# Softmax per head in whole-head instructions, its mask added by TensorE in the first two batches, a weight's sign by a 16-bit VectorE operation, and two PSUM banks for group 0

## The chip, the core and the metric

One core of one Trainium2 chip runs the whole program. The metric is the device time of one execution in microseconds (us). The engines are named as in the profile: PE (TensorE matmuls), PEld (its weight loads), DVE (VectorE), ACT (ScalarE), POOL (GpSimd) and SP (SyncE, which here issues every DMA).

## What is computed

Windowed attention over 8 batches, 8 heads, 576 positions and 64 values per head, then a gated MLP on all 4608 tokens. Half of the heads see the last 32 positions, the others every fourth of the last 128.

```python
scores = scale * np.matmul(q, k.transpose(0, 1, 3, 2))
rel = pos[:, None] - pos[None, :]
mask_plain = (rel >= 0) & (rel < window)
mask_dil = (rel >= 0) & (rel < window * dilation) & (rel % dilation == 0)
scores = np.where(masks[None, :, :, :], scores, -1000000000.0)
scores = scores - np.max(scores, axis=-1, keepdims=True)
attn = np.exp(scores)
attn = attn / (np.sum(attn, axis=-1, keepdims=True) + 1e-09)
x = np.matmul(attn, v)                      # then tokens x 512
h = x @ w_in                                # 512 -> 2048
g = h * (1.0 / (1.0 + np.exp(-1.702 * h)))
out = g @ w_out                             # 2048 -> 512
```

## The kernel before

The MLP runs over nine groups of 512 tokens: one for each batch (`main[0]` to `main[7]`) and one for the tails of all batches (`rest`). In each group, `up(f)` for f = 0 to 15 makes 128 of the 2048 hidden values (12 matmuls of 128x512, line 437), `tanh` on ACT (L445), `gate` on DVE (L448), `hi_g` and `lo_g` split the result into two parts, and `down(f)` adds it into four accumulators (12 matmuls, lines 473, 474 and 477). Every product is made from three: high times high, low times high, high times low. `up` writes a PSUM bank `hp`; only the first two steps of group 0 use `sp0` and `sp1` instead (L431). So `up(f+1)` has to wait until `gate` of f has read the bank.

The weights come as 64-bit floats. `decode` (L210) turns one block of them into a high and a low fp32 part: a DMA into one of five cells, three ACT instructions (`value` L235, `low` L236, `sign` L237), a shift (L239) and an add (L241) on DVE, then the high part (a copy, ACT or DVE) and the low part (a subtraction, DVE or POOL). There are 32 blocks, two for each f, and all are decoded while group 0 runs.

`attention(b, c)` handles two heads (a = 0, 1) of one batch, c = 0 to 3. `scores` (L278) makes 20 windows of 32 queries by 64 keys into a PSUM tile of 128 partitions by 5 by 64 for each head. `exponents` (L295) then runs five times for each head, on 128x64 elements: a DVE instruction that scales, adds the mask and takes the maximum (L298, with a second instruction that reads the maximum out), and an ACT Exp that also sums (L301, with a second one that reads the sum out). `weights` divides by the sum (`pr` times `sm`, DVE or POOL) and transposes on DVE; `spread` copies the result into `bt` (copies, or DMAs for batch 1 and for half of batch 0); `product` (L353) multiplies with v on PE; `drain_x` writes the tokens' vectors. Batch 0 is handled before group 0 starts, batch b + 1 beside group b.

The order is made in advance. Every piece of work is added to a `Plan` with its cost on the engines that could do it, its urgency and what it reads and writes; `ordered` (L63) then replays time with these costs and takes, at each moment, the most urgent piece that could start, on the cheapest engine that could start it. Each engine runs its part in just that order: an instruction that waits holds all that stand behind it. In the first 30 us of the plan, `warm` matmuls of zeros (L546) fill PE's planned idle time. Pools, DVE and SP follow the same list.

Of the kernel before, what the change touches and what calls it, by code (L numbers as in the profile page):

```python
# [115 lines left out]
def tile_windowed_attention_then_gated_mlp(  # L116
# [61 lines left out]
    V.memset(mask[0:32, 0, 0:32], NEG)  # L178

# [30 lines left out]
    def decode(n, urgency):  # L210
# [17 lines left out]
        freed = () if f < NF - 4 or n % 2 == 0 else ("bt1",)  # L228
        low, top = (raw.bitcast(U32).rearrange("p (n t) -> p n t", t=2)[:, :, j] for j in range(2))
        sign = raw.bitcast(F16).rearrange("p (n t) -> p n t", t=4)[:, :, 1]  # L230
# [4 lines left out]
        add({ACT: 0.56}, urgency, lambda e: A.activation(value, f32(top), AF.Copy, scale=2.0 ** -112), (R,), (E,))  # L235
        add({ACT: 0.56}, urgency, lambda e: A.activation(low, low, AF.Copy, scale=2.0 ** -29), (R,), (R + "l",))  # L236
        add({ACT: 0.56}, urgency, lambda e: A.activation(sign, f32(top), AF.Copy, scale=2.0 ** -112),  # L237
            (R,), (R + "l",))
        add({DVE: -0.335}, urgency, lambda e: V.tensor_scalar(  # L239
            out=word, in0=word, scalar1=3, scalar2=None, op0=ALU.logical_shift_left), (), (E,))  # L240
        add({DVE: -0.61}, urgency, lambda e: V.tensor_tensor(out=word, in0=word, in1=low, op=ALU.add),  # L241
            (R + "l",), (E, *freed))
        add({ACT: 0.56, DVE: -0.34}, urgency, lambda e: copy(e, hi, value), (E,), (key,))
        add({DVE: -0.61, POOL: 1.35}, urgency, lambda e: pair(e, lo, value, f32(hi), ALU.subtract), (E,), (key,))
# [4 lines left out]
    def attention(b, c, urgency):  # L249
# [4 lines left out]
        y = (i + 1) % 2 if b == 0 else 0  # L254
# [20 lines left out]
        places = [f"acc{(2 * i + a) % 4}" if b == 0 else f"sp{a}" for a in range(2)]  # L275
        chained = b >= FIRST

        def scores(e, heads):  # L278
            for a in heads:
                u["sp", a] = bank([P, QT, W], places[a], f"sp_{i}_{a}")  # L280
            for t in range(QT):
                for a, j in [(a, j) for a in heads for j in range(min(4, S // 32 - 4 * t))]:
                    g, rows = 4 * t + j, slice(D * a, D * a + D)
                    dst, keys = u["sp", a][32 * j:32 * j + 32, t], u["qk"][rows, 1]
                    for w in (0, 32) if g == 0 else (0,):
                        n = 32 if g == 0 else W
                        at = max(32 * g - 32, 0)
                        T.matmul(dst[:, w:w + n], u["qk"][rows, 0, 32 * g:32 * g + 32], keys[:, at:at + n],  # L288
                                 start=True, stop=True, tile_position=(D * a, 32 * j))

        for heads in ((0,), (1,)) if b < FIRST else ((0, 1),):
            add({PE: 0.5 * len(heads)}, urgency - 1.0e5, lambda e, heads=heads: scores(e, heads),
                (f"qk{z}", "product") if chained else (f"qk{z}",), [places[a] for a in heads], 1.0 if b else 0.0)

        def exponents(a, t):  # L295
            n = min(P, S - P * t)
            box, key = pr[0:n, a, t], f"{i % 2}{a}.{t}"
            add({DVE: 0.15}, urgency, lambda e: V.tensor_tensor_reduce(  # L298
                out=box, in0=u["sp", a][0:n, t], in1=mask[0:n, t if dil or t == 0 else QT - 1], scale=-0.125, scalar=-NEG,
                op0=ALU.add, op1=ALU.min, accum_out=mx[0:n, a, t:t + 1]), (places[a],), (f"pr{key}", f"mx{key}"))  # L300
            add({ACT: 0.33}, urgency, lambda e: A.activation(  # L301
                box, box, AF.Exp, bias=mx[0:n, a, t:t + 1], scale=-1.0, accum_out=sm[0:n, a, t:t + 1]),
                (f"mx{key}",), (f"pr{key}", f"sm{key}"))

        def weights(hs):

            n, heads = hs.stop - hs.start, range(hs.start, hs.stop)
            boxes = [f"{i % 2}{a}.{t}" for a in heads for t in range(QT)]
            sums, probs = [f"sm{k}" for k in boxes], [f"pr{k}" for k in boxes]
            for a in heads:  # L310
                for t in range(QT):
                    exponents(a, t)
# [3 lines left out]
            for a in heads:  # L316
                add({POOL: 0.69, DVE: -0.41}, urgency, lambda e, a=a: pair(
                    e, pr[:, a], pr[:, a], sm[:, a, :, None].broadcast_to([P, QT, W]), ALU.mult),
                    sums, [f"pr{i % 2}{a}.{t}" for t in range(QT)])
# [5 lines left out]
        def spread():  # L325

            for m in (4, 5, 6, 7, 0, 1, 2, 3):
# [15 lines left out]
                if b == 1 or y:  # L343
                    costs = {DMA: 82}
                else:
                    costs = {ACT: 0.49, DVE: -0.33}
                add(costs, urgency, work, [f"ct{i % 2}{prev}{a}" for a in (0, 1)], (f"bt{y}{m}", f"spread{i}.{m}"))

        for hs in (slice(0, 1), slice(1, 2)) if b < FIRST else (slice(0, 2),):
            weights(hs)  # L350
# [21 lines left out]
        def drain_x(hf):  # L372
# [35 lines left out]
    class Group:  # L408
# [20 lines left out]
        def up(self, f):  # L429
            hps = self.hps  # L430
            place = ("sp0", "sp1")[f] if self is main[0] and f < 2 else "hp"  # L431
# [31 lines left out]
            if self is main[0]:  # L463
                lows[POOL] = 1.23
# [122 lines left out]
```

## Time and profile before

| | |
|---|---|
| median of 3 runs | 927.82 us (927.69 to 929.02) |
| the profiled execution | 927.5 us |
| its span, first to last instruction | 925.6 us |
| PE busy | 901.4 us, 97% |
| DVE busy | 476.4 us, 51% |
| ACT busy | 402.0 us, 43% |
| POOL busy | 45.2 us, 5% |
| mean granted TensorE clock | 0.994 |

Shares over the whole span mix two very different parts. Up to about 161 us the weights are decoded, batch 0 and 1 are attended and group 0 runs; from there on, PE works without a gap. So the page's table by slices, and tables by stretch, are read before the shares. A busy PE is not PE at its peak: matmuls overlap, so the distance from start to start tells what one costs.

### The profile page before, as it was taken

The page shows a single profiled execution, that of the slowest core. Times are in us where ns is not written, and L with a number is a line of the kernel's source. Part 1 is how long each engine was busy: PE and PEld are TensorE (multiplying, and loading weights), DVE is VectorE, ACT ScalarE, POOL GpSimd, SP SyncE. Part 2 cuts the span into 40 slices and gives each one's busy share as a digit, 9 for nine tenths or more (in the row PEclk, how much of TensorE's full clock was granted, in tenths as well). Part 3 has the DMA queues.
Part 4 walks back from the last instruction along what each step waited for, and adds up shares of the span by engine and source line. Part 5 has one row for each costly group of instructions (what it writes and reads, how often), then busy time and mean ns, then how long its engine had stood idle before and what let it go on. Part 6 is the DMA issues. An engine that isn't in the chain of part 4 may idle for free.

```text
span 925.6 us, 17159 instructions
## 1 busy us (share of the span) xinstructions
PE 901.4 (97%) x6721; PEld 726.0 (78%) x6726; DVE 476.4 (51%) x1529; ACT 402.0 (43%) x1187; POOL 45.2 (5%) x41
## 2 busy tenths in 40 slices
PE   8798889999999999999999999999999999999997
PEld 4476676888888888888888888888888888888886
DVE  7786785656365436653656346544653333333332
ACT  6999995545255215541545144522551121122111
POOL 1023120000000000000000000000000000000000
PEclk9989999999999999999999999999999999999999
DMA  7566543121031102210221002200200010001002
GB/s 261 177 218 201 156 139 134 41 81 41 16 112 40 56 1 86 67 52 4 72 58 64 15 26 86 82 15 0 86 2 1 1 45 1 1 1 46 0 1 46
DMA packets 25185, 58.60 MB, mean 63 GB/s; under 512 B 6992, under 2 KB 8720, under 8 KB 25104
## 3 DMA queue, kind: packets, MB, share of 16 engines
q1 hardware_dynamic: 25104, 57.50, 19.2%
q8 instruction: 53, 0.87, 0.4%
q14 instruction: 28, 0.23, 0.1%
HBM read 46.14 MB, written 9.44 MB: 60 GB/s over the span
## 4 chain that ended last, share of the span: by engine, by line
PE 88%; ACT 8%; DVE 2%; POOL 1%; issue 0%; DMA 0%; DVEq 0%; ACTq 0%
PE hp_m L437 35%; PE acc_m L473 12%; PE acc_m L477 12%; PE acc_m L474 12%; PE hp_r L437 5%; PE av L361 4%; PE sp L288 3%; ACT cell L237 2%; PE acc_r L477 2%; PE acc_r L474 2%; PE acc_r L473 2%; ACT words L235 1%; ACT second L237 1%; ACT cell L236 1%; ACT pr L301 1%; ACT g_m L445 1%
## 5 line engine op out<-in xcount | busy, mean ns | idle before, releaser
L437 PE MATMUL hp_m<-xh,wih 128*128 128x512 f32 x512 | 204.8, 400 | 10.2 <-DVE g_m L448 9.5
L448 DVE SCALAR_TENSOR_TENSOR g_m<-g_m,hp_m 128x512 f32<-128x512 f32 x128 | 87.9, 687 | 240.7 <-ACT g_m L445 239.7
L473 PE MATMUL acc_m<-gh,woh 128*128 128x512 f32 x512 | 202.5, 395 | 2.9 <-DVE gh L196 2.9
L437 PE MATMUL hp_m<-xh,wil 128*128 128x512 f32 x512 | 200.3, 391 | 0.3 <-DVE wil L201 0.3
L474 PE MATMUL acc_m<-gh,wol 128*128 128x512 f32 x512 | 200.3, 391 | 0.0
L437 PE MATMUL hp_m<-xl,wih 128*128 128x512 f32 x512 | 200.2, 391 | 0.0
L445 ACT ACTIVATE g_m<-hp_m 128x512 f32<-128x512 f32 x128 | 76.8, 600 | 262.0 <-PE hp_m L437 261.2
L477 PE MATMUL acc_m<-gl,woh 128*128 128x512 f32 x512 | 143.6, 393 | 0.0
L301 ACT ACTIVATE pr<-pr,mx 128x64 f32<-128x64 f32 (+1 forms) x320 | 106.8, 336 | 61.8 <-DVE mx L298 61.7
L437 PEld LDWEIGHTS hp_m<-xh,wih 128*128 128x128 f32 x512 | 96.5, 188 | 34.6 <-DVE g_m L448 12.5
L473 PEld LDWEIGHTS acc_m<-gh,woh 128*128 128x128 f32 x512 | 96.6, 189 | 24.1 <-DVE gh L196 3.3
L437 PEld LDWEIGHTS hp_m<-xl,wih 128*128 128x128 f32 x512 | 96.5, 188 | 21.4 <-DVE xl L201 0.9
L477 PEld LDWEIGHTS acc_m<-gl,woh 128*128 128x128 f32 x512 | 95.9, 189 | 20.5
L474 PEld LDWEIGHTS acc_m<-gh,wol 128*128 128x128 f32 x512 | 96.7, 189 | 19.6
L437 PEld LDWEIGHTS hp_m<-xh,wil 128*128 128x128 f32 x512 | 96.6, 189 | 19.4 <-DVE wil L201 0.6
L201 DVE TENSOR_TENSOR gl<-g_m,gh 128x512 fp32r<-128x512 f32 x126 | 89.4, 710 | 17.3 <-ACT gh L194 8.8
L298 DVE CUSTOM_DVE_ANT_0 pr<-sp,mask 128x64 f32<-128x64 f32 (+1 forms) x320 | 50.3, 213 | 46.9 <-PE sp L288 46.6
L301 ACT ACTIVATION_READ_ACCUMULATOR pr<-pr,mx 128x1 f32 (+1 forms) x320 | 60.4, 189 | 0.0
L194 ACT ACTIVATE bt<-ct 32x320 f32<-32x320 f32 (+1 forms) x97 | 44.5, 459 | 33.9 <-DVE ct L321 32.3
L196 DVE CAST gh<-g_m 128x512 fp32r<-128x512 f32 x111 | 47.3, 426 | 8.8
L194 ACT ACTIVATE xm<-av 128x256 f32<-128x256 f32 (+2 forms) x56 | 28.0, 506 | 39.7 <-PE av L361 39.7
L445 ACT ACTIVATE g_r<-hp_r 128x512 f32<-128x512 f32 x16 | 9.6, 600 | 73.3 <-PE hp_r L437 73.3
(93 smaller groups left out, 852.5 us busy)
## 6 DMA issues: line engine op xcount, KB each, us to landing
qk<-qk_dram SPq DMA_DIRECT2D x16, 576.0 KB, 4.3
out_dram<-ost_m SPq DMA_DIRECT2D x32, 256.0 KB, 2.0
second<-qk_dram SPq DMA_DIRECT2D x13, 576.0 KB, 3.7
cell<-wi_dram SPq DMA_DIRECT2D x11, 512.0 KB, 4.6
cell<-wo_dram SPq DMA_DIRECT2D x11, 512.0 KB, 4.2
v<-vp_dram SPq DMA_DIRECT2D x17, 320.0 KB, 3.0
second<-vp_dram SPq DMA_DIRECT2D x13, 320.0 KB, 3.0
second<-wi_dram SPq DMA_DIRECT2D x5, 512.0 KB, 4.1
```

What stands on the lines that cost most here:

```text
L194: A.activation(dst, src, AF.Copy, scale=scale)
L196: V.tensor_copy(out=dst, in_=src)
L201: (V if e == DVE else G).tensor_tensor(out=dst, in0=a, in1=b, op=op)
L298: add({DVE: 0.15}, urgency, lambda e: V.tensor_tensor_reduce(out=box, in0=u["sp", a][0:n, t], in1=mask[0:n, t if dil or t == 0 else QT - 1 ...
L301: add({ACT: 0.33}, urgency, lambda e: A.activation(box, box, AF.Exp, bias=mx[0:n, a, t:t + 1], scale=-1.0, accum_out=sm[0:n, a, t:t + 1]), ...
L361: T.matmul(av[D * a:D * a + D, col:col + hi - lo], u["v"][:, a, t], bt[:, lo // 32:hi // 32, a, t], start=m == 0, stop=m == 2, skip_group_ ...
L437: T.matmul(hps[f], st[:, f, c], mv[:, c], start=c == 0 and k == 0, stop=c == NC - 1 and k == 2)
L445: A.activation(self.g32, hps[f], AF.Tanh, scale=0.851)
L448: V.scalar_tensor_tensor(out=self.g32, in0=self.g32, scalar=1.0, in1=hps[f], op0=ALU.add, op1=ALU.mult)
L473: T.matmul(self.acc[j], woh[:, f, cols], gh, start=f == 0, stop=False)
L474: T.matmul(self.acc[j], wol[:, f, cols], gh, start=False, stop=False)
L477: T.matmul(self.acc[j], woh[:, f, P * j:P * j + P], self.g[f][1], start=False, stop=f == NF - 1)
```

## The change

**Softmax.** `exponents` now runs once for each head. In batches 0 and 1 (b below `FIRST` = 2) PE adds the mask: a matmul of an identity matrix with the mask (`ident`, 128x320, bf16) opens the scores' tile and the scores accumulate onto it. DVE then takes the five maxima (a reduction over 128x5x64), subtracts them, ACT does one Exp over 128x320, and DVE sums by a second reduction. From batch 2 on there is no such matmul; DVE adds the mask from PSUM in two instructions for each head (128x256 and 64x64) first. A second mask `plain` and `ident` are made at the start, three of the small copies there move to ACT, and POOL makes `ident`.

**Sign.** The sign of a weight may be written either by ACT, as before, or by DVE as a 16-bit AND of every fourth half-word; the plan chooses. In the order that it made, 5 of 32 are on DVE and 27 remain on ACT.

**Banks.** All `up` steps of group 0 alternate between `sp1` and `hp`. For that, both heads of batch 1 use `sp0`, one after the other, and the bank's second user waits for DVE to have read the first.

**Costs and order.** Nearly all costs in the plan are other numbers, batch 1 is more urgent (40 + 14c in place of 50 + 20c), and the scores of a batch's second head are added after the first head's softmax. So the order changes nearly everywhere in the first 160 us.

```diff
+    mask, plain = fixed([P, QT, W], BF16, "mask"), fixed([P, QT, W], BF16, "plain")
+    zeros, ident = fixed([P, P], BF16, "zeros"), fixed([P, P], BF16, "ident")
...
+        def take_sign(e):
+            if e == ACT:
+                A.activation(halves[:, :, 1].bitcast(F16), f32(top), AF.Copy, scale=2.0 ** -112)
+            else:
+                V.tensor_scalar(out=halves[:, :, 1], in0=halves[:, :, 3], scalar1=0x8000, scalar2=None,
+                                op0=ALU.bitwise_and)
...
-        add({ACT: 0.56}, urgency, lambda e: A.activation(sign, f32(top), AF.Copy, scale=2.0 ** -112),
-            (R,), (R + "l",))
+        add({DVE: -0.43, ACT: 1.35}, urgency, take_sign, (R,), (R + "l",))
...
-        places = [f"acc{(2 * i + a) % 4}" if b == 0 else f"sp{a}" for a in range(2)]
+        places = [f"acc{(2 * i + a) % 4}" if b == 0 else "sp0" if b == 1 else f"sp{a}" for a in range(2)]
...
+                if masked:
+                    T.matmul(u["sp", a], ident, mine, start=True, stop=False, skip_group_check=True)
...
-        def exponents(a, t):
...
-            add({DVE: 0.15}, urgency, lambda e: V.tensor_tensor_reduce(
...
-            add({ACT: 0.33}, urgency, lambda e: A.activation(
-                box, box, AF.Exp, bias=mx[0:n, a, t:t + 1], scale=-1.0, accum_out=sm[0:n, a, t:t + 1]),
...
+        def exponents(a):
...
+            if not masked:
+                for n, tiles, cost in ((P, slice(0, QT - 1), 0.35), (D, slice(QT - 1, QT), 0.15)):
+                    add({DVE: cost}, urgency, lambda e, n=n, tiles=tiles: pair(
+                        e, box[0:n, tiles], u["sp", a][0:n, tiles], mine[0:n, tiles], ALU.add),
+                        (places[a],), (f"pr{key}",))
+            add({DVE: 0.40}, urgency, lambda e: V.tensor_reduce(
+                out=mx[:, a], in_=sp(), axis=AX.X, op=ALU.max), (*held, f"pr{key}"), (f"mx{key}",))
+            add({DVE: 0.42}, urgency, lambda e: pair(
+                e, box, sp(), mx[:, a, :, None].broadcast_to([P, QT, W]), ALU.subtract),
+                (*held, f"mx{key}"), (f"pr{key}",))
+            add({ACT: 0.42}, urgency, lambda e: A.activation(box, box, AF.Exp, scale=0.125), (), (f"pr{key}",))
+            add({DVE: 0.40}, urgency, lambda e: V.tensor_reduce(
+                out=sm[:, a], in_=box, axis=AX.X, op=ALU.add), (f"pr{key}",), (f"sm{key}",))
...
-            place = ("sp0", "sp1")[f] if self is main[0] and f < 2 else "hp"
+            place = ("sp1", "hp")[f % 2] if self is main[0] else "hp"
```

What DVE has in its queue for the first two heads of batch 0 (`pr` the probabilities, `mx` the maxima, `sm` the sums, `sp` the scores in PSUM), before, where five pairs such as the first two make one head:

```order
L298 ISA pr_78,mx_80<-sp_1_162,mask 64x64
L298 ISA mx_80 64x1
L313 TENSOR_SCALAR sm_82<-sm_82 128x5
L315 RECIPROCAL sm_82<-sm_82 128x5
L298 ISA pr_79,mx_81<-sp_0_203,mask 128x64
L298 ISA mx_81 128x1
L201 TENSOR_TENSOR pr_78<-pr_78,sm_82 128x320
```

and with the change:

```order
L319 TENSOR_REDUCE mx_80<-sp_0_143 128x5
L319 TENSOR_REDUCE mx_80<-sp_1_164 128x5
L204 TENSOR_TENSOR pr_78<-sp_0_143,mx_80 128x320
L204 TENSOR_TENSOR pr_78<-sp_1_164,mx_80 128x320
L325 TENSOR_REDUCE sm_82<-pr_78 128x5
L319 TENSOR_REDUCE mx_81<-sp_0_196 128x5
L334 TENSOR_SCALAR sm_82<-sm_82 128x5
```

Ten instructions of a head have become three on DVE, and the division by the sum has left DVE's queue for POOL's in batch 0.

What ACT has there, before (the Exps of one head are the first two rows):

```order
L301 ACTIVATE pr_79,sm_83<-pr_79,mx_81 128x64 x4
L301 ACTIVATE pr_79,sm_83<-pr_79,mx_81 64x64
L301 ACTIVATE pr_78,sm_82<-pr_78,mx_80 128x64 x4
L301 ACTIVATE pr_78,sm_82<-pr_78,mx_80 64x64
L194 ACTIVATE bt<-ct_85 32x320 x3
L235 ACTIVATE words_120<-cell_117 128x512
```

and with the change, from its first activation:

```order
L184 ACTIVATE plain<-mask 128x320
L190 ACTIVATE mask<-mask 32x64
L324 ACTIVATE pr_78<-pr_78 128x320 x2
L324 ACTIVATE pr_79<-pr_79 128x320 x2
L324 ACTIVATE pr_78<-pr_78 128x320 x2
L246 ACTIVATE words_121<-cell_118 128x512
L247 ACTIVATE cell_118<-cell_118 128x512
```

The first weights are now decoded behind six Exps, where twenty-five stood before them.

On PE, where the first `down` (`acc_m`) follows the first two `up` steps (`hp_m_0`, `hp_m_1`), before:

```order
L437 MATMUL hp_m_1_635<-xl,wih 128x512
L473 MATMUL acc_m_0_679<-gh_72,woh 128x512
L474 MATMUL acc_m_0_679<-gh_72,wol 128x512
L288 MATMUL sp_0_683<-qk_645 32x32 x2
L288 MATMUL sp_0_683<-qk_645 32x64 x17
L473 MATMUL acc_m_1_706<-gh_72,woh 128x512
```

and with the change:

```order
L457 MATMUL hp_m_1_608<-xl,wih 128x512
L294 LDWEIGHTS ident
L294 MATMUL sp_0_640<-plain,ident 128x320
L302 MATMUL sp_0_640<-qk_605 32x32 x2
L302 MATMUL sp_0_640<-qk_605 32x64 x17
L493 MATMUL acc_m_0_663<-gh_72,woh 128x512
```

The scores of batch 1's first head, with the mask's matmul, have moved ahead of the first `down`.

## Rows read from the trace of the kernel before

**Rows 1.** Busy time by stretch: PE, PEld, DVE, ACT, POOL (us, count), PEclk, DMA share, GB/s

```profile
6.00:42.90 36.90, 32.15 (x449) 19.84 (x450) 28.45 (x151) 34.43 (x121) 1.99 (x2) 1.00 0.69 235
42.90:148.50 105.60, 95.58 (x716) 74.20 (x717) 80.94 (x241) 98.30 (x211) 24.64 (x16) 0.95 0.52 171
...
45.10:51.50 6.40, 6.40 (x50) 4.76 (x51) 5.41 (x17) 6.40 (x10) 0.00 (x0) 0.53 0.27 83
81.95:85.40 3.45, 3.45 (x8) 2.75 (x9) 2.95 (x6) 3.45 (x16) 0.00 (x0) 0.52 0.85 282
...
161.30:920.00 758.70, 758.67 (x5383) 622.16 (x5384) 358.41 (x1100) 260.51 (x836) 14.78 (x13) 1.00 0.11 37
```

**Rows 2.** PE's waits: who for whom, us in total, times, longest

```profile
PE hp_m L437 <- DVE g_m L448: 9.5, 7, 3.0
```

**Rows 3.** Timeline of PE: start, duration, what, count, idle before and its releaser

```profile
45.10 0.79 PE L473 MATMUL acc_m<-gh,woh 128*128 128x512 f32 x1 [2.90 <-DVE gh L196]
...
51.56 0.40 PE L437 MATMUL hp_m<-xh,wih 128*128 128x512 f32 x1
...
52.34 0.76 PE L288 MATMUL sp<-qk 64*32 64x32 f32 x38
...
81.95 0.79 PE L437 MATMUL hp_m<-xh,wih 128*128 128x512 f32 x1 [3.02 <-DVE g_m L448]
...
153.85 0.82 PE L361 MATMUL av<-bt,v 128*64 128x128 f32 x12
...
161.33 0.50 PE L437 MATMUL hp_m<-xh,wih 128*128 128x512 f32 x1 [1.65 <-DVE g_m L448]
```

**Rows 4.** Timeline of DVE: gates f0 and f15, first head's softmax, beside a POOL op

```profile
6.22 0.23 DVE L298 CUSTOM_DVE_ANT_0 pr<-sp,mask 128x64 f32<-128x64 f32 x1 [0.53 <-PE sp L288]
...
6.80 0.21 DVE L298 CUSTOM_DVE_ANT_0 pr<-sp,mask 64x64 f32<-64x64 f32 x1
...
42.92 0.68 DVE L448 SCALAR_TENSOR_TENSOR g_m<-g_m,hp_m 128x512 f32<-128x512 f32 x1
...
72.97 0.68 DVE L201 TENSOR_TENSOR gl<-g_m,gh 128x512 fp32r<-128x512 f32 x1
...
76.05 0.41 DVE L196 CAST woh<-words 128x512 fp32r<-128x512 f32 x1
...
148.47 0.69 DVE L448 SCALAR_TENSOR_TENSOR g_m<-g_m,hp_m 128x512 f32<-128x512 f32 x1
```

**Rows 5.** Timeline of ACT: Exps in a row, signs in a row, and a wait

```profile
8.15 0.33 ACT L301 ACTIVATE pr<-pr,mx 128x64 f32<-128x64 f32 x1
...
8.49 0.33 ACT L301 ACTIVATE pr<-pr,mx 128x64 f32<-128x64 f32 x1
...
44.34 1.32 ACT L237 ACTIVATE second<-second 128x512 f16<-128x512 f32 x1
45.41 1.41 ACT L237 ACTIVATE cell<-cell 128x512 f16<-128x512 f32 x1
...
77.65 0.67 ACT L235 ACTIVATE words<-second 128x512 f32<-128x512 f32 x1 [1.27 <-POOL wol L201]
```

**Rows 6.** Groups by line and shape: count | busy us, mean ns of one | idle before

```profile
L201 DVE TENSOR_TENSOR pr<-pr,sm 128x320 f32<-128x320 f32 x54 | 24.9, 488 | 0.6
L196 DVE COPY bt<-ct 32x320 f32<-32x320 f32 x103 | 32.5, 316 | 1.9
L239 DVE TENSOR_SCALAR words<-words 128x512 uint32<-128x512 uint32 x32 | 14.5, 462 | 2.3 <-ACT words L235 2.3
L194 ACT ACTIVATE bt<-ct 32x320 f32<-32x320 f32 x79 | 37.0, 469 | 33.5 <-DVE ct L321 32.3
```

**Rows 7.** Timeline of POOL, the columns as in rows 3

```profile
66.68 1.30 POOL L201 TENSOR_TENSOR wil<-words,wih 128x512 fp32r<-128x512 f32 x1 [2.09 <-ACT wih L194]
72.89 5.98 POOL L201 TENSOR_TENSOR wol<-words,woh 128x512 fp32r<-128x512 f32 x2 [4.91 <-ACT woh L194]
```

**Rows 8.** Timeline of PE: a run of the matmuls of zeros

```profile
16.41 4.26 PE L546 MATMUL idle<-zeros 128*128 128x512 bf16 x19 [0.16 <-issue]
```

More of the change, by code (lines that the diff above doesn't have):

```diff
@@ L242, in decode @@
             (R + "l",), (E, *freed))
-        add({ACT: 0.56, DVE: -0.34}, urgency, lambda e: copy(e, hi, value), (E,), (key,))
-        add({DVE: -0.61, POOL: 1.35}, urgency, lambda e: pair(e, lo, value, f32(hi), ALU.subtract), (E,), (key,))
+        add({ACT: 0.62, DVE: -0.42}, urgency, lambda e: copy(e, hi, value), (E,), (key,))
+        add({DVE: -0.70, POOL: 1.7}, urgency, lambda e: pair(e, lo, value, f32(hi), ALU.subtract), (E,), (key,))
     spare = [second.bitcast(F32).rearrange("p j n -> p (j n)"), xm.rearrange("p c n -> p (c n)"),
@@ L316, in weights @@
             for a in heads:
-                add({POOL: 0.69, DVE: -0.41}, urgency, lambda e, a=a: pair(
+                add({POOL: 0.73, DVE: -0.48}, urgency, lambda e, a=a: pair(
                     e, pr[:, a], pr[:, a], sm[:, a, :, None].broadcast_to([P, QT, W]), ALU.mult),
-                    sums, [f"pr{i % 2}{a}.{t}" for t in range(QT)])
+                    sums, (f"pr{i % 2}{a}",))
             for half in (0, 1):
@@ L341, in work @@
                         copy(e, dst, src)
[L343 to L346, printed above, removed]
+                costs = {DMA: 82} if b == 1 or y else {ACT: 0.49, DVE: -0.33}
                 add(costs, urgency, work, [f"ct{i % 2}{prev}{a}" for a in (0, 1)], (f"bt{y}{m}", f"spread{i}.{m}"))
-        for hs in (slice(0, 1), slice(1, 2)) if b < FIRST else (slice(0, 2),):
-            weights(hs)
+        for heads in ((0,), (1,)) if b < FIRST else ((0, 1),):
+            add({PE: 0.5 * len(heads)}, urgency - 1.0e5, lambda e, heads=heads: scores(e, heads),
+                (f"qk{z}", "product") if chained else (f"qk{z}",), [places[a] for a in heads], 1.0 if b else 0.0)
+            weights(slice(heads[0], heads[-1] + 1))
         spread()
@@ L458, in up @@
             H_, L_ = f"gh{f % 2}", f"gl{f % 2}"
[L459 to L462 removed]
+            add({ACT: 0.60}, -10.0, tanh, (place,), ("g32",))
+            add({DVE: 0.69}, -10.0, gate, (place,), ("g32",))
+            add({ACT: 0.62, DVE: -0.42}, -10.0, hi_g, ("g32",), (H_, L_))
+            lows = {DVE: -0.70}
             if self is main[0]:
[L464 removed]
+                lows[POOL] = 1.35
             add(lows, -10.0, lo_g, ("g32", H_), (L_,))
@@ L532, in tile_windowed_attention_then_gated_mlp @@
                 for c in range(NC):
-                    attention(1, c, 50.0 + 20.0 * c)
+                    attention(1, c, 40.0 + 14.0 * c)
+                for n in range(2 * NF - 8, 2 * NF):
+                    decode(n, 25.0 + 2.3 * n)
             if last:
@@ L543, in warm @@
     def warm(e):
+        if 0 in main[0].hps:
+            return
         if not idle:
             idle["bank"] = bank([P, GT], "sp1", "idle")
-        T.matmul(idle["bank"], zeros[:, 0:P], zeros, start=True, stop=True)
+        T.matmul(idle["bank"], zeros, zeros[:, None, :].broadcast_to([P, GT // P, P]), start=True, stop=True)
     for work, e in plan.ordered(warm, WARM):
```

58 lines of the change are left out of this document (25 added, 33 removed).

## The prediction

> **What bounds the kernel now.** I read the table by stretch first. From 161.3 us on PE is busy for 758.67 of 758.70 us at full clock [rows 1]: whatever DVE or ACT do there is hidden behind PE as long as no result is late. The change gives PE no less to do, so time can only be won before 161 us. There the same table says who is full: between the gates of f0 (42.9) and f15 (148.5) ACT is busy 98.30 of 105.60 us, 93%, DVE 80.94 us, 77%, and PE's clock falls to 0.95; from 6 to 42.9 us ACT has 34.43 of 36.90 us, again 93%, DVE 28.45 us, 77% [rows 1]. PE waits because of it: seven times, 9.5 us in all, `up` waits for a gate that has yet to empty the one bank [rows 2], and once the first `down` waits 2.90 us [rows 3]. Behind the two longest waits (2.90 and 3.02 us) the granted clock drops from 2.4 to 1.2 GHz: 0.53 for 6.40 us and 0.52 for 3.45 us [rows 1, 3], which costs 0.47 x 6.40 = 3.0 and 0.48 x 3.45 = 1.7 us. So PE loses 9.5 + 2.9 + 3.0 + 1.7 = 17.1 us between 42 and 161 us; 15.4 of it lies before the gate of f15, since the last wait (1.65 at 161.33) comes later. That is the most that can be won there. The rest of the start is the chain through batch 0.
>
> **What the change does to ACT.** Five Exps of a head follow each other at (8.49 - 8.15) = 0.34 us, their sums included [rows 5]: 1.7 us a head. One Exp on 128x320 is not in the trace; the copy of 32x320 takes 0.47 [rows 6], a 64-wide Exp alone 0.33 [rows 5]; I take 0.47. So a head saves 1.2 us, and 16 heads of batches 0 and 1 save 19 us. A sign takes 45.41 - 44.34 = 1.07 us [rows 5]; by the order five leave ACT: up to the gate of f0 it has one more than before (the queue is further ahead), between the gates six fewer. ACT then has about 34.4 - 8 x 1.2 + 1.1 = 26 us before the gate of f0 and 98.3 - 8 x 1.2 - 6 x 1.07 = 82 us between the gates, some casts more. ACT stops being the limit.
>
> **What it does to DVE.** A head's five instructions follow each other at (6.80 - 6.22) / 4 = 0.145 us [rows 4], 0.73 us a head. They were cheap. In their place stand a reduction, a subtraction and a second reduction over 320 elements. A reduction is not in the trace: the nearest rows on 320 elements are the copy, 0.32, and `pr` times `sm`, 0.49 [rows 6]; I take 0.40, in the middle, and 0.41 for the subtraction, which overlaps its neighbours as the product does. A 16-bit sign is bounded by nothing at all and, from above, by ACT's 1.07; the nearest row is the shift on 512 elements, 0.46 [rows 6], and I take 0.45. Counted in the order up to the gate of f0: out go 40 pairs (-5.8) and two low parts (-1.2); in come 16 reductions (+6.4), 8 subtractions for 7 products that POOL now makes (+0.4), two signs (+0.9), two copies, a word's add and a cast (+1.6). That is +2.3, so 28.45 + 2.3 = 30.8 us. Between the gates: out 40 pairs (-5.8), two low parts, three casts and one add (-2.8); in 18 reductions (+7.2; two are batch 2's), 18 products, subtractions and mask sums for 5 (+4.6), three signs (+1.4). That is +4.6, so 85.5 us. Together 116.3 us, and **DVE is the fullest engine** of the first 150 us.
>
> **PE's own additions.** A mask matmul has 320 columns; a matmul of zeros on 512 takes 4.26 / 19 = 0.224 us [rows 8], so 0.14, and up to 0.3 where the kinds of matmul change; I take 0.2. Eight lie between the matmuls of zeros of the start, where PE waits anyway, and eight in group 0: 1.6 us. Two banks take no time and remove the condition that `up(f+1)` waits for the gate of f; what comes late next is `gh` for the `down` that follows, one step of ACT or DVE behind the gate. Scores of batch 1 now share `sp0`: the second head's wait for DVE's subtraction, and in PE's queue `up` and `down` matmuls stand behind them; between the two in the order stand 21 matmuls of group 0, 4.8 us, against some 3 us of DVE. I cost that at nothing; without this cover each of four would cost a microsecond or two. The copies at the start and `ident` lie before the first q and k, at nothing; if they come late, 0.5 us. From batch 2 on, DVE gets about 2 us more per attention (two sums, two reductions, one subtraction, twice, for ten pairs), 24 x 2 = 48 us on 358 of 759 [rows 1]: 54%, still half idle, and hidden as long as the gates are not late.
>
> **The sum.** I need the share that DVE can reach when it limits: its own 77% was reached with ACT in the way, and 93% is what ACT reached as the limit [rows 1]. Its queue is in order and ACT (82 of some 98 us between the gates), POOL and PE all take turns with it, so I take 87%. Its first softmax instruction comes at 6.5 (6.22 before [rows 4], and two mask matmuls). Gate of f15: 6.5 + 116.3 / 0.87 = 140.2 us. Before it was at 148.5 [rows 4], and the product of batch 1's last heads came after it, twice 0.82 [rows 3], where the new order has it before; so 150.1 is what to compare with. The wait of 1.65 at the border of group 0 [rows 3] mostly goes (1.5), since batch 1 ends earlier. Gain: 150.1 + 1.5 - 140.2 = 11.4 us. PE allows it: without its losses, with the masks and that product it needs 105.6 - 15.4 + 1.6 + 1.6 = 93.4 us between the gates, and DVE takes 85.5 / 0.87 = 98.3. The profiled execution is 927.5 us (span 925.6), 0.3 under the median of 927.82; 927.5 - 11.4 = 916.1. **Forecast 916 us.**
>
> **Rivals.** *PE becomes the limit again.* DVE reaches 93%: the gate of f0 at 6.5 + 30.8 / 0.93 = 39.6, then PE's 93.4, 133.0 in all; gain 18.6, **909 us**. For it: two banks and costs in the plan that are close to the trace's; against it: PE, DVE and ACT would all be above 85% at once.
>
> *POOL is locked out.* A POOL operation that takes 1.30 us elsewhere [rows 7] lasted from 72.89 until about 77.6 (its twin makes up the 5.98), and ACT's `words` waited 1.27 us for it [rows 5, 7], ahead of PE's wait at 81.95. DVE had seven instructions without idle time from 72.97 to 76.46 then (the first and the last in [rows 4]), and POOL ended about one operation's time later. The new order has 17 such operations on POOL between the gates in place of 14, beside a fuller DVE. One such block cost 3.0 + 1.7 = 4.7 us on PE; two that are not there now would leave 916 + 9.4 = **925 us**. The Trainium skill ("SBUF — State Buffer", Who interferes with whom) says that DVE's two-input SBUF operations and its fast copy modes take a port pair as an exclusive lock from GpSimd, and that reductions on trn2 never do; the trace agrees with the block, and no run here shows a reduction. By that rule the new instructions of batch 0 and 1 leave POOL alone and this rival loses most of its price.
>
> *DVE at its old share.* If the chain reduction, subtraction, Exp, reduction, with a trip to ACT inside, lets DVE wait as often as before, it stays at 77%: the gate of f15 at 6.5 + 116.3 / 0.77 = 157.5, 5.9 us later than 151.6, so **933 us**, slower than before. The point from which it decides is 116.3 / (151.6 - 6.5) = 80%. For it: each head has four steps on DVE with ACT between; against it: the order puts other heads and decoding between them.
>
> *The change doesn't do what it says.* For the sign this is nearly so: 27 of 32 stay on ACT, by the order. It is in the sum.
>
> **How the numbers follow.** Forecast (87%, from 84 to 90%: 912 to 921) 0.60; PE the limit 0.14; POOL locked out 0.14; DVE at its old share 0.12. Below 80% it is slower, and one per cent of share is 1.5 us. The range of 910 to 925 holds the forecast, most of the first rival and of the second: DVE from 82 to 91%. A measurement can tell about 0.2%, 1.9 us, from no change. Faster: 0.60 + 0.14 + most of 0.14, 0.84; within 0.2%: 0.05; slower: 0.11.
>
> **What would show it.** In the changed kernel's table by stretch DVE should be at 85 to 90% and ACT below 90% until the gate of f15, which should lie near 140 us; PE's waits for `g_m` should be nearly gone and waits for `gh` should be short, no stretch at clock 0.5 behind the first `down`; a reduction should take 0.35 to 0.45 us; from the second group on PE should be without gaps as before. The prediction is wrong if reductions take 0.6 us or more (16 before the gate of f0, 34 in all: 0.2 x 34 = 7 us), if PE waits in groups 1 to 7, which nothing in the sum allows for, or if DVE's queue waits on POOL's products in batch 0.

## The result, and the profile after

The changed kernel takes **917.41 us** (median of 4 runs, 916.97 to 917.55) against 927.85 us before: ratio 0.9884, 95% interval 0.9867 to 0.9901. The profiled execution is 917.38 us with a span of 915.7 us, 9.9 us under the span before. The time is close to the forecast of 916; the reason the forecast gave for its size is not the right one, as the runs below show.

The table by stretch answers rows 1: from 6 us to the gate of f0, between the gates, a short stretch ahead of the first gate, the border to group 1, and the rest. The line after the dots is the border of the kernel before, which rows 1 did not hold.

```profile
6.00:43.27 37.27, 34.16 (x453) 20.95 (x450) 30.39 (x93) 25.03 (x47) 11.19 (x12) 0.95 0.65 229
43.27:143.57 100.30, 98.64 (x836) 76.28 (x835) 86.74 (x188) 86.16 (x142) 24.15 (x19) 1.00 0.58 192
36.70:41.10 4.40, 4.11 (x28) 3.09 (x29) 4.36 (x9) 4.40 (x10) 0.91 (x2) 0.61 0.52 188
143.57:148.66 5.09, 4.99 (x22) 3.80 (x21) 4.76 (x13) 2.24 (x5) 1.29 (x1) 1.00 0.01 3
150.00:900.00 750.00, 750.00 (x5347) 615.17 (x5346) 385.93 (x833) 209.93 (x427) 17.70 (x18) 1.00 0.12 38
...
148.47:160.59 12.12, 10.73 (x134) 7.96 (x132) 3.93 (x25) 5.68 (x15) 0.00 (x0) 1.00 0.45 151
```

Between the gates PE is now busy for 98.64 of 100.30 us at full clock, where it had waits and half clock before [rows 1 to 3]. ACT fell from 98.30 us there [rows 1] to 86.16. The border is 5.09 us long in place of 12.12.

PE's waits in the changed kernel, to be set beside rows 2: the 9.5 us for `g_m` are gone, and what is left above 0.5 us lies ahead of the first gate.

```profile
PE av L381 <- DVE xl L204: 2.7, 2, 1.8
...
PE acc_m L493 <- ACT cell L247: 0.4, 1, 0.4
PE acc_m L493 <- DVE gh L199: 0.4, 1, 0.4
PE acc_m L493 <- ACT gh L197: 0.3, 1, 0.3
```

PE's timeline there, answering rows 3, and DVE's two gates, answering rows 4:

```profile
32.38 1.60 PE L381 MATMUL av<-wol,xm 128*64 128x128 f32 x24 [0.85 <-DVE xl L204]
...
36.71 0.33 PE L381 MATMUL av<-bt,xr 128*64 128x128 f32 x2 [1.83 <-DVE xl L204]
...
44.33 0.31 PE L294 MATMUL sp<-plain,ident 128*128 128x320 bf16 x1
```

```profile
43.27 0.68 DVE L468 SCALAR_TENSOR_TENSOR g_m<-g_m,hp_m 128x512 f32<-128x512 f32 x1
...
143.57 0.67 DVE L468 SCALAR_TENSOR_TENSOR g_m<-g_m,hp_m 128x512 f32<-128x512 f32 x1
```

The new operations, from the groups by line and shape (answering rows 6; the prices that the prediction had to bound):

```profile
L325 DVE TENSOR_REDUCE sm<-pr 128x5 f32<-128x320 f32 x64 | 29.5, 480 | 6.0 <-ACT pr L324 3.5
L324 ACT ACTIVATE pr<-pr 128x320 f32<-128x320 f32 x64 | 29.0, 469 | 66.1 <-DVE pr L204 65.8
L239 ACT ACTIVATE cell<-cell 128x512 f16<-128x512 f32 x19 | 26.0, 1367 | 0.1
L204 POOL TENSOR_TENSOR wol<-words,woh 128x512 fp32r<-128x512 f32 x7 | 9.6, 1367 | 32.7 <-ACT woh L197 21.8 <-DVE woh L199 11.0
L204 DVE TENSOR_TENSOR pr<-sp,mx 128x320 f32<-128x320 f32 x16 | 7.6, 478 | 0.1
L294 PE MATMUL sp<-plain,ident 128*128 128x320 bf16 x8 | 2.7, 341 | 0.4 <-ACT plain L184 0.4
L241 DVE TENSOR_SCALAR cell<-cell 128x512 uint16<-128x512 uint16 x3 | 2.3, 754 | 0.1
```

Where the 9.9 us came from, by the gates of the two profiles: the gate of f0 is 0.35 us later (43.27, 42.92 before). From there to the gate of f0 of group 1 it is 148.66 - 43.27 = 105.39 us in place of 160.59 - 42.92 = 117.67, a gain of 12.28. Group 1 loses 0.4 (a gate-to-gate time of 93.62 in place of 93.26), from its last gate to the last gate of all both kernels take 661.85 us, and the tail behind that gate loses 1.7 us. Of these, 0.45 lie ahead of the last four stores, whose issue begins 3.89 us behind the last gate in place of 3.44; the other 1.2 us lie between that issue and the end. Before and after, the issue of the four on SP, and the table of DMA in slices of 0.53 us:

```profile
919.14 2.95 SPq L495 DMA_DIRECT2D out_dram<-ost_r  x4
GB/s 0 0 0 0 0 0 0 0 0 0 0 0 0 31 0 0 0 0 0 0 0 0 0 0 0 0 0 0 0 139 290 286 290 287 288 289 127 0 0 0
```

```profile
908.02 3.36 SPq L515 DMA_DIRECT2D out_dram<-ost_r  x4
GB/s 0 0 0 0 0 0 0 0 161 217 215 202 229 208 226 215 217 108 0 0 0 0 0 0 0 0 0 0 0 0 0 0 0 0 0 0 0 0 0 0
```

The same four transfers run at some 215 GB/s in place of 288. From group 1's last gate to the end, the kernels below that are derived from the changed one take 672.8 to 673.4 us, those derived from the kernel before 671.7 to 672.6. Why the rate is lower was not tried and stays open.

### The profile page after: what moved, and what is told of

Its sections match the earlier page's. It is cut to its first block, busy times and chain, and to the rows that moved or that the text cites. A ratio compares the mean times of both kernels' runs of the same rounds, so it can differ in the third digit from the quotient of the medians.

```text
span 915.7 us, 16236 instructions
## 1 busy us (share of the span) xinstructions
PE 902.4 (99%) x6738; PEld 726.3 (79%) x6738; DVE 514.1 (56%) x1140; ACT 329.0 (36%) x628; POOL 57.1 (6%) x60
## 4 chain that ended last, share of the span: by engine, by line
PE 92%; ACT 2%; DMA 2%; DVE 2%; SPq 0%; issue 0%; DVEq 0%; ACTq 0%
PE hp_m L457 37%; PE acc_m L493 13%; PE acc_m L497 12%; PE acc_m L494 12%; PE hp_r L457 5%; PE av L381 4%; PE sp L302 3%; PE acc_r L497 2%; PE acc_r L493 2%; PE acc_r L494 2%; DMA qk<-qk_dram 1%; DMA cell<-wo_dram 1%; ACT cell L239 1%; SPq L360 0%; ACT cell L247 0%
## 5 line engine op out<-in xcount | busy, mean ns | idle before, releaser
L204 DVE TENSOR_TENSOR gl<-g_m,gh 128x512 fp32r<-128x512 f32 x123 | 87.2, 709 | 13.4 <-ACT gh L197 6.1
L197 ACT ACTIVATE bt<-ct 32x320 f32<-32x320 f32 (+1 forms) x102 | 47.2, 462 | 36.5 <-DVE ct L342 35.1
L324 ACT ACTIVATE pr<-pr 128x320 f32<-128x320 f32 x64 | 29.0, 469 | 66.1 <-DVE pr L204 65.8
L199 DVE CAST gh<-g_m 128x512 fp32r<-128x512 f32 x97 | 42.3, 437 | 9.3 <-PE acc_m L494 0.9
L468 DVE SCALAR_TENSOR_TENSOR g_r<-g_r,hp_r 128x512 f32<-128x512 f32 x16 | 11.0, 688 | 54.4 <-ACT g_r L465 54.4
L204 POOL TENSOR_TENSOR pr<-pr,sm 128x320 f32<-128x320 f32 x23 | 18.3, 800 | 335.4 <-DVE sm L336 329.1
```

Source lines behind the costliest of these rows:

```text
L197: A.activation(dst, src, AF.Copy, scale=scale)
L199: V.tensor_copy(out=dst, in_=src)
L204: (V if e == DVE else G).tensor_tensor(out=dst, in0=a, in1=b, op=op)
L324: add({ACT: 0.42}, urgency, lambda e: A.activation(box, box, AF.Exp, scale=0.125), (), (f"pr{key}",))
L468: V.scalar_tensor_tensor(out=self.g32, in0=self.g32, scalar=1.0, in1=hps[f], op0=ALU.add, op1=ALU.mult)
```

## The experiments

The columns give the median, the ratio to the kernel before, and from the profiled execution the first `up` matmul, the gate of f0, the time from gate f0 to gate f15, and the border from there to group 1's first gate.

| kernel | us | ratio (95%) | first up | gate f0 | f0 to f15 | border |
|---|---|---|---|---|---|---|
| before | 927.8 | 1 | 31.1 | 42.9 | 105.6 | 12.1 |
| after | 917.4 | 0.988 (0.987-0.990) | 30.6 | 43.3 | 100.3 | 5.1 |
| x1_dve_plus | 917.65 | 0.989 (0.986-0.991) | 30.0 | 42.5 | 101.2 | 5.1 |
| x2_pe_plus | 920.66 | 0.992 (0.989-0.994) | 33.1 | 45.8 | 102.2 | 5.1 |
| e9_mask_dve | 917.74 | 0.990 (0.988-0.992) | 33.4 | 45.9 | 100.0 | 5.1 |
| e1_one_bank | 919.09 | 0.990 (0.987-0.993) | 33.2 | 45.7 | 99.9 | 6.0 |
| e2_old_softmax | 916.05 | 0.987 (0.985-0.989) | 31.8 | 40.6 | 101.1 | 5.1 |
| e5_sign_act | 920.71 | 0.993 (0.990-0.996) | 30.8 | 45.5 | 105.1 | 5.1 |
| e8_costs_banks | 927.98 | 1.000 (0.998-1.001) | 33.0 | 37.4 | 118.0 | 4.5 |
| e3_banks_only | 923.35 | 0.996 (0.994-0.997) | 32.1 | 43.8 | 98.9 | 13.9 |
| e4c_urgency | 921.89 | 0.993 (0.991-0.996) | 31.8 | 43.0 | 107.2 | 4.4 |
| e4_costs_only | 921.49 | 0.994 (0.992-0.996) | 34.0 | 38.4 | 108.8 | 4.8 |
| e4b_numbers | 935.02 | 1.009 (1.007-1.010) | 32.3 | 36.7 | 108.6 | 19.4 |
| e7_old_costs | 934.16 | 1.008 (1.005-1.011) | 30.6 | 43.9 | 96.7 | 25.2 |

**Which engine sets the time between the gates?** Two kernels keep the changed order to the last instruction and only make one engine's work longer.

```diff
-                out=sm[:, a], in_=box, axis=AX.X, op=ALU.add), (f"pr{key}",), (f"sm{key}",))
+                out=sm[:, a], in_=box, axis=AX.X, op=ALU.add) for _ in range(3 if b == 1 else 1)],
```

> The changed kernel in the same order; each head of batch 1 makes its sum three times in place of once (the plan isn't told): 16 reductions more on DVE between the gates, 16 x 0.40 = 6.4 us. If DVE's queue sets the time there, as the prediction has it (87% reachable): 6.4 / 0.87 = 7.4 us, 924 to 925 us. If PE sets it: DVE goes from 84.0 to 90.4 of 98.0 us in the stretch and the time stays within 1 us of 917.4.

```diff
                     T.matmul(u["sp", a], ident, mine, start=True, stop=False, skip_group_check=True)
+                    for _ in range(3 if b == 1 else 0):
+                        T.matmul(u["sp", a], zeros, mine, start=False, stop=False, skip_group_check=True)
```

> The changed kernel in the same order; each head of batch 1 adds three matmuls of zeros of 128x320 onto its scores (the plan isn't told): 24 x 0.14 = 3.4 us more on PE between the gates (0.14 from 0.224 us for 512 columns, rows 8). If PE sets the time there: 920.5 to 921.5 us. If DVE's queue sets it, as the prediction has it: PE has some 5 us to spare there by the prediction's sum, and the time stays within 1 us of 917.4.

Both came out as expected if PE sets the time: more DVE work left the time where it was (917.65), more PE work cost 3.2 us (920.66). The table of the stretch from 42 to 140 us of x1_dve_plus:

```profile
42.00:140.00 98.00, 95.88 (x822) 73.50 (x822) 90.78 (x198) 84.25 (x137) 23.06 (x18) 1.00 0.57 193
```

DVE took 90.78 of 98.00 us, 93%. Between the gates this kernel needs 0.9 us more than the changed one (101.2 against 100.3), where 7.4 were expected if DVE's queue set the time. So DVE was not the limit at 87%, as the forecast had it. In x2_pe_plus the stretch between the gates is 1.9 us longer (102.2), and PE is busy for 101.42 us of it: 2.8 us more work, of which 0.9 went into what had been idle time. The rest of what its profile shows is a start that is 2.5 us later (gate of f0 at 45.8), which the last section comes back to. So PE sets the time there, but not to the last microsecond.

**Softmax and signs: what unloads ACT.** Four kernels, all with the new numbers and two banks, make a square: with both (after), with either, with neither. Three of them have an order that was planned for them; e5_sign_act keeps that of the changed kernel.

e2_old_softmax puts the old pair of instructions back for batches 0 and 1, without the mask matmul; the plan then puts 10 signs on DVE:

```diff
+            if b < FIRST:
+                for t in range(QT):
...
+                    add({DVE: 0.15}, urgency, lambda e, n=n, t=t, box=box: V.tensor_tensor_reduce(
...
+                    add({ACT: 0.33}, urgency, lambda e, n=n, t=t, box=box: A.activation(
...
+                return
```

> The changed kernel, but batches 0 and 1 use the old softmax (five pairs of instructions and five Exps for each head, no mask matmul); two banks, costs and the choice for the sign stay. By the plan 10 signs are now on DVE in place of 5. Theory 1 (ACT's load made the waits): ACT has 19 us more of Exps, less 5 signs x 1.07, and is at 93% again; 8 to 10 us are lost, 925 to 927 us. Theory 2 (two banks and the order made the gain): 917 to 920 us, since PE is also rid of the mask matmuls in group 0 (8 x 0.3 = 2.4 us).

e5_sign_act keeps the changed order and writes all signs on ACT:

```diff
-            if e == ACT:
+            if True:
```

> The changed kernel in the same order, with the five signs of DVE written by ACT at their place in the order (the plan isn't told): DVE has 5 x 0.69 = 3.5 us less, ACT 5 x 1.07 = 5.4 us more, of it three signs between the gates. If PE sets the time between the gates: within 1 us of 917.4, or 1 us less if the two signs ahead of the gate of f0 held up DVE's xl there. If the signs on DVE are worth their place, as the prediction's ACT and DVE sums have it: 919 to 922 us.

e8_costs_banks is the kernel before with the edits of e3_banks_only and e4_costs_only (both below), so with neither:

> The kernel before with two parts of the change, the plan's numbers (as e4_costs_only) and the two banks (as e3_banks_only), and without the other two: old softmax, no mask matmul, every sign on ACT. If the order and the banks made the gain: the start of e4_costs_only (gate of f0 near 38 us) and PE without gaps between the gates, less the mask matmuls, some 98 us: 912 to 916 us. If unloading ACT is needed (new softmax, signs on DVE): ACT at 94 of 98 us holds PE up as in e4_costs_only, 920 to 923 us.

Neither: 927.98, nothing gained. Softmax alone: 920.71, in the range for signs that are worth their place. Signs alone (ten): 916.05. Both: 917.41. Two of these lie outside what was expected, e2 below both of its ranges and e8 above both. Inside the square either part alone gives most of the gain, and **with the signs on DVE the new softmax adds nothing**: e2, with the old one, is at least as fast as the changed kernel. e2 also shows that PE, DVE and ACT can all be above 90% at once, which the prediction held against its first rival (stretch from 42 to 140 us, and below it that of e3_banks_only, which comes later):

```profile
42.00:140.00 98.00, 96.28 (x818) 73.17 (x817) 88.95 (x259) 90.85 (x204) 16.57 (x13) 1.00 0.59 197
42.00:140.00 98.00, 92.33 (x704) 71.42 (x703) 77.91 (x234) 96.64 (x210) 22.96 (x16) 0.98 0.55 182
```

That unloading ACT is needed, as the prediction said, these runs don't show. ACT is at 93% in e2, the share that it had before [rows 1], and PE has lost its long waits all the same. And e4_costs_only, further down, has neither the new softmax nor a sign on DVE, and only one bank; it takes 921.49 us, within a microsecond of softmax alone. e8_costs_banks is that kernel with the second bank. Between the gates (e8 first, then e4) PE is idle for as long in both, 10.8 and 10.6 us, and most of what e8 loses there is clock, at 0.94 in place of 1.00 with nearly the same number of PE instructions:

```profile
37.41:155.44 118.03, 107.27 (x836) 81.39 (x836) 95.39 (x283) 105.98 (x228) 7.73 (x6) 0.94 0.53 177
38.39:147.20 108.81, 98.17 (x833) 76.38 (x834) 91.72 (x275) 104.73 (x228) 10.38 (x8) 1.00 0.60 192
```

Over the whole span the mean clock is 0.991 to 0.995 in the ten runs of e8 and 0.994 to 0.999 in the four of e4. So what softmax alone is worth, 7 us beside e8 and under one beside e4, stays open.

How a sign hurts is seen in e5_sign_act: two of the five moved signs and a `gh` on ACT, then PE, then the table of the two stretches behind its waits:

```profile
38.66 1.44 ACT L239 ACTIVATE second<-second 128x512 f16<-128x512 f32 x1
...
121.30 1.39 ACT L239 ACTIVATE cell<-cell 128x512 f16<-128x512 f32 x1
...
129.12 0.68 ACT L197 ACTIVATE gh<-g_m 128x512 fp32r<-128x512 f32 x1
```

```profile
41.90 0.80 PE L457 MATMUL hp_m<-xh,wih 128*128 128x512 f32 x1 [2.71 <-DVE xl L204]
129.85 0.79 PE L493 MATMUL acc_m<-gh,woh 128*128 128x512 f32 x1 [1.96 <-ACT gh L197]
```

```profile
41.90:46.00 4.10, 4.10 (x10) 3.24 (x11) 1.67 (x3) 4.10 (x7) 0.80 (x1) 0.50 0.86 304
129.85:133.00 3.15, 3.15 (x7) 2.50 (x8) 3.15 (x7) 3.15 (x5) 0.00 (x0) 0.51 0.42 89
```

The moved sign at 38.66 stands ahead of ACT's last `xh`, so `xl` is late and PE waits 2.71 us (0.28 in the changed kernel), then runs at 1.2 GHz for 4.1 us. The one at 121.30 and one at 117.01 leave ACT's queue late, and the `gh` at 129.12, which cost PE 0.34 us in the changed kernel, costs 1.96, with the same end. (This profile is of the slowest of the four runs, 924.35 us.) In e8_costs_banks it is a sign, too, that holds the first `down`, and half clock follows (PE's row, then the stretch behind it). In e4_costs_only, the second row of PE, the same sign holds the same matmul for as long, and no half clock follows:

```profile
38.71 0.47 PE L472 MATMUL acc_m<-gh,woh 128*128 128x512 f32 x1 [2.02 <-ACT cell L237]
39.68 0.47 PE L473 MATMUL acc_m<-gh,woh 128*128 128x512 f32 x1 [2.04 <-ACT cell L237]
```

```profile
38.70:46.00 7.30, 7.29 (x54) 5.39 (x55) 5.39 (x18) 5.45 (x12) 0.00 (x0) 0.56 0.61 196
```

ACT has 87.5 of the 98 us from 42 to 140 us in e8, no more than in e2. So in these profiles it is not ACT's share that costs but which `gh`, `cell` or `xh` stands behind a 1.07 us sign in its queue, and whether the clock falls behind the wait. One caution on this corner: e8 also keeps one `bt` buffer for batch 1, where the changed kernel and e2 use two (`y = (i + 1) % 2 if b < FIRST`, a part of the change not spoken of until here); none of its longer waits is for `bt`.

**The bank.**

```diff
-            place = ("sp1", "hp")[f % 2] if self is main[0] else "hp"
+            place = "sp1" if self is main[0] and f == 0 else "hp"
```

> The changed kernel, but in group 0 only f=0 uses sp1; from f=1 on all steps of up use the one bank hp, as in the kernel before. The plan makes its order anew; signs stay 5 on DVE. Theory 1 (ACT's load made the waits): with ACT unloaded the gate comes in time, waits for g_m of at most 1.5 us in all, 917.4 to 919 us. Theory 2 (the second bank removes the waits): the waits for g_m come back, 5 to 9.5 us in all as in rows 2, 922 to 927 us, with a stretch at half clock behind any wait of some 3 us.

One wait for `g_m` of 0.6 us came back, 0.9 us at the border, and nothing between the gates (99.9 us): the first theory's waits. The median is 1.7 us higher with runs from 915.68 to 920.31, and the profiled one starts late. In the changed kernel the second bank is worth about a microsecond. Alone in the kernel before it is worth more (the places and the order of batch 1's scores go with it, and the matmuls of zeros end with group 0's first `up`, as in the changed kernel):

```diff
-            place = ("sp0", "sp1")[f] if self is main[0] and f < 2 else "hp"
+            place = ("sp1", "hp")[f % 2] if self is main[0] else "hp"
```

> The kernel before with one part of the change, the banks: all steps of up in group 0 alternate between sp1 and hp, both heads of batch 1 use sp0. Old softmax, old costs, signs on ACT. If the one bank made the waits: the 9.5 us for g_m (rows 2) and the half clock behind the longest of them (1.7 us) go, 917 to 919 us. If the order does (a plan that takes a sign for 0.56 us where ACT needs 1.07 gives ACT too much): the waits only move to gh, 925 to 928 us.

923.35 us, between the two ranges. The waits for `g_m` shrink to one of 1.6 us, and the gates are 98.9 us apart, although ACT is busy for 96.6 of 98 us there. That is no longer than in the changed kernel, but with less in it: PE is busy for 93.20 us between these gates, against 98.64. Of the 6.7 us won between the gates, 1.8 are given back at the border and 0.9 ahead of the first gate.

**The plan's numbers and urgencies.** e4_costs_only has both in the kernel before, e4b_numbers the cost numbers alone, e4c_urgency the urgencies alone:

```diff
-                    attention(1, c, 50.0 + 20.0 * c)
+                    attention(1, c, 40.0 + 14.0 * c)
+                for n in range(2 * NF - 8, 2 * NF):
+                    decode(n, 25.0 + 2.3 * n)
```

> The kernel before with one part of the change, the plan's numbers: the new costs (a sign 1.35 on ACT in place of 0.56, and so on) and batch 1's and the last weights' new urgencies. No instruction is another one: old softmax, signs on ACT, one bank. If the order made the gain: 917 to 920 us, with waits for g_m of under 2 us. If softmax or banks made it: ACT stays at 93% between the gates, 925 to 928 us.

> As e4_costs_only, but with the new cost numbers alone: batch 1 keeps its urgency of 50 + 20c and the last eight weights their place. If the cost numbers carry the gain of e4_costs_only: within 2 us of it. If the urgencies carry it: 925 to 928 us.

> The kernel before with the new urgencies alone (batch 1 at 40 + 14c, the last eight weights behind it), its old cost numbers, old softmax, signs on ACT, one bank. If batch 1's end is what e4b_numbers lost (its next group starts 19.4 us after the gate of f15, 4.8 in e4_costs_only) and the urgencies mend that alone: 919 to 923 us. If they help only together with the numbers: 926 to 930 us.

The urgencies do it: 921.89 alone, as expected for that case; 921.49 with the numbers, between the two ranges; 935.02 with the numbers alone, above both. What they mend is the border, 4.4 us in place of 12.1, since batch 1 is done before group 1 needs it; e4c still has waits for `g_m` of 6.6 us in all. In e4b batch 1 comes last, and PE stands for it:

```profile
PE av L361 <- DMA bt<-ct: 6.2, 1, 6.2
```

> The changed kernel without the plan's new numbers: the old costs wherever both kernels have the operation, the old urgencies, the sign on ACT at 0.56; the new softmax and the two banks stay. If the order made the gain: 923 to 928 us, with the waits for a late ACT back. If softmax and banks made it, as the prediction has it: 917 to 919 us.

In e7_old_costs the last eight weights are decoded ahead of batch 1 again, while batch 1's second `bt` still lies in the last four `wol`: it overwrites them, so this kernel computes something else, and batch 1 waits until those weights are done. Its border of 25.2 us says nothing on costs. Nor do its 96.7 us between the gates, since PE is busy for only 91.42 us in them and the rest is at the border. The run shows only that this part of the change can't be taken out alone.

So the parts don't add. Banks alone -4.4 us and urgencies alone -5.9 would make -10; with the numbers, and without less work on ACT, the sum is nothing (e8). Banks and urgencies without the numbers were not tried, so what part the numbers have in e8's loss stays open; nor were softmax or sign tried alone in the kernel before.

**The mask back on DVE in batch 1**, in the changed order:

```diff
-                if masked:
+                if b == 0:
                     T.matmul(u["sp", a], ident, mine, start=True, stop=False, skip_group_check=True)
...
+            def top(e):
+                for n, tiles in ((P, slice(0, QT - 1)), (D, slice(QT - 1, QT))) if b == 1 else ():
+                    pair(DVE, box[0:n, tiles], u["sp", a][0:n, tiles], mine[0:n, tiles], ALU.add)
```

> The changed kernel in the same order, but in batch 1 DVE adds the mask from PSUM (128x256 and 64x64 for each head, as from batch 2 on) ahead of its reduction, and the mask matmul is left out there (the plan isn't told): PE has 8 x 0.3 = 2.4 us less in group 0, DVE 8 x 0.55 = 4.4 us more. If PE sets the time between the gates, as x1_dve_plus and x2_pe_plus say: about 915.0 us, under both kernels. If the longer chain of each head on DVE comes to the path (the bank sp0, which the second head waits for): 917 to 919 us.

917.74 us: in the second range, and a miss for "PE sets the time". Between the gates PE is busy for 97.42 us in place of 98.64, 1.2 us less for eight matmuls, and its short waits grow from 1.7 to 2.6 us in all, so that only 0.3 us is won there; the profile also began late (first `up` at 33.4). "PE sets the time" holds within a microsecond or two; below that, the next wait takes over.

No version beats both kernels clearly. e2_old_softmax, at 916.05 us, is 1.4 us under the changed kernel, with ratios whose intervals overlap.

## Why the prediction came out right, and where it was wrong

That the total comes within 1.4 us of the forecast is luck: the limit was another engine, and errors of several us on both sides of the last gate cancelled.

**Right in part: what bounds before.** PE's losses were the thing to win, and the waits for `g_m` and the half-clock stretches behind them are gone. That ACT's load made them is not shown: e2 has ACT at 93% without them, and e3, e4 and e4c keep every ACT instruction and still gain 4 to 6 us. What e5 shows in its place is that the place of a few long ACT instructions in the queue is enough to bring such waits back.

**Right: most prices.** The Exp takes 0.469 us (0.47), the subtraction 0.478 and the reduction 0.48; in the timeline they follow each other at about 0.40, as the sum had it. DVE has 30.39 us from 6 us to the gate of f0 (30.8) and 86.74 between the gates (85.5). ACT has 25.03 (26) and 86.16 (82).

**Wrong: the price of a sign on DVE.** 0.754 us by its duration, 0.54 to 0.62 from its start to the next one's where nothing else is waited for (as from 115.98 to 116.60), against 0.45 taken from the 32-bit shift. And its worth was mis-sized the other way: the prediction counted a sign as 1.07 us of ACT's time, and moving the five back to ACT costs 3.3 us (e5), since two of them, in its profile, hold up `xh` and `gh`.

**Wrong: the step "DVE can reach 87% and limits".** x1_dve_plus reached 93% with 0.9 us more between the gates. The gate of f15 came at 143.57, not 140.2, and PE was busy for all but 1.66 us up to it. The term that failed is PE's need, forecast at 93.4 us and measured at 98.64. The work that the new order has between the gates is not one product of 1.6 us more. By the count of PE's matmuls it is the product (24, 1.7 us), batch 2's first scores (76, 1.1 us) and 12 of `up` and `down` (2.7 us at 0.23 each), 5.5 us in all; six of these twelve are `up` of f1, which before came ahead of the gate of f0. The mask's price was not the fault: 0.15 each by e9_mask_dve's busy time, at most 0.36 by the starts (44.33 to the scores, which show at 44.69), against 0.2. Before, PE was busy for 95.58 us between the gates [rows 1], of it 4.7 us lost to the half clock; 95.58 - 4.7 + 5.5 + 8 x 0.2 = 98.0.

**Wrong, but made up for.** The border became 7.0 us shorter, where 3.1 were counted. The forecast's 11.4 us were 1.0 from an earlier gate of f0 (6.5 + 30.8 / 0.87 = 41.9, 42.92 before) and 10.4 behind it; measured are -0.35 and 12.28, then -0.4 and -1.7 in what follows, 9.9 in all. The earlier gate did not come (43.27): `xl` for the last head of batch 0 is late, PE waits 0.85 and 1.83 us, and its clock is 0.61 behind that. With the new numbers the old softmax has that gate at 37 to 41 us (40.6 in e2), which suggests that the whole-head form costs batch 0 some 3 us, where the prediction counted 2.3 us of DVE time at a higher share; e2 also has other signs on DVE, so this is argued. For the 1.7 us of the tail the prediction had no term.

**The rivals.** "PE becomes the limit again" was the right mechanism; its price of 909 us used a PE need 5 us too low and an early gate of f0. POOL was hardly held up: its `wol` takes 1.37 us on average and `wil` 1.46, where 1.30 was the undisturbed time [rows 7]. The Trainium skill ("SBUF — State Buffer", Who interferes with whom) has reductions leave POOL alone; the trace agrees: at 50.35 us POOL's `gl` takes 1.29 us while DVE begins two reductions and nothing else. "DVE at its old share" would have shown as DVE near 77%; it is at 86.

**What was missed altogether.** The urgencies of batch 1, which the prediction named only as a reason why the order changes, are worth 5.9 us alone in the kernel before, the most of the parts tried there: they turn the border from 12.1 into about 5 us.

## What to carry to other kernels

Where a planner fixes the order, ask of each long instruction on a side engine not only how full that engine is, but which short instruction that PE waits for stands behind it: moving five signs back to ACT cost 3.3 us. Before an engine is named as the limit, load it: the same order with 6.4 us more on one engine, and with 3.4 on the other, told what shares of 86% could not. Nor is a full engine the limit because it is full: ACT was at 93% in the kernel before and in e2_old_softmax, 12 us faster. And when work moves across the mark that a sum is made to (here the last gate), count it on both sides of the mark.

## What the runs showed of the hardware that was not expected

**PE at half its rate at a granted clock of 1.00.** Six matmuls of zeros at the start take 2.7 us or 1.5 us, and the switch comes at another time in each execution of what are the same instructions up to there: by 5 us in x1_dve_plus, near 10 in the changed kernel, near 15 in x2_pe_plus. The runs of six, in this order, from the timelines of PE, and the table of x2_pe_plus for 7 to 10 and 10 to 13 us:

```profile
6.55 1.47 PE L571 MATMUL idle<-zeros 128*128 128x512 bf16 x6
```

```profile
7.65 2.58 PE L570 MATMUL idle<-zeros 128*128 128x512 bf16 x6
...
11.91 1.47 PE L570 MATMUL idle<-zeros 128*128 128x512 bf16 x6
```

```profile
7.55 2.74 PE L572 MATMUL idle<-zeros 128*128 128x512 bf16 x6
...
13.31 2.60 PE L572 MATMUL idle<-zeros 128*128 128x512 bf16 x6
```

```profile
7.00:10.00 3.00, 3.00 (x26) 1.27 (x19) 1.77 (x4) 0.87 (x2) 0.21 (x1) 1.00 1.02 398
10.00:13.00 3.00, 3.00 (x77) 2.06 (x77) 1.18 (x5) 0.00 (x0) 0.00 (x0) 1.00 1.03 409
```

The granted clock reads 1.00 throughout, and PE is busy without a gap from 4.7 us on in x2_pe_plus, so neither that row nor an idle PE tells when the switch comes. The Trainium skill ("TensorE: Matmul & The Clock Gate", Part 1) says that the number of matmuls at the lower clock at a kernel's start differs from run to run, and warns of the trace's clock events; these runs agree, and the rate at the start can be half while the row of the clock reads 1.00. Since the changed order leaves PE no idle time there (3.00 of 3.00 us), the first `up` shifts by it: 30.0, 30.6 and 33.1 us. That is as large as the differences between several kernels of the table, and a reason to compare them by stretch rather than by the median alone; in the one profile of e1_one_bank, its slowest run, the matmuls of zeros are still slow at 13.30 us (2.66 us for six) and the first `up` comes at 33.2; that the whole spread of that kernel (915.68 to 920.31) is this shift is argued, not shown.

**A wait's length alone doesn't tell what the clock does.** Behind waits of 1.83, 1.96 and 2.02 us the clock fell (0.61, 0.51, 0.56 in the stretches above), while e4_costs_only kept 1.00 behind the 2.04 us shown beside e8's 2.02, and e2_old_softmax behind a wait of 2.15 us (the row of PE, and the table of 36 to 44 us):

```profile
37.91 0.50 PE L473 MATMUL hp_m<-xh,wih 128*128 128x512 f32 x1 [2.15 <-ACT xr L200]
```

```profile
36.00:44.00 8.00, 5.71 (x57) 3.83 (x58) 6.71 (x13) 8.00 (x16) 1.29 (x1) 1.00 0.85 305
```

**A 16-bit operation was slower than a 32-bit one.** 512 half-words at a stride of four took 754 ns; the shift of 512 whole words took 462 [rows 6]. The stride and the width changed together, so which of them costs was not tried.
